# Loading and casting the wide pieces of w_in in parts, with three tiles of the first h side by side

## The chip, the cores and the metric

The kernel runs on one core of one Trainium2 chip. The metric is device microseconds of one execution, as the hardware reports it. The profile of an execution has a "span", from the first to the last instruction, that is about 2.1 us shorter than the reported time.

## The reference

Softmax attention without the score matrix, then a dense layer with exact gelu:

```
q_s = softmax(q, over head_dim);  k_s = softmax(k, over sequence)
kv  = einsum('bhsd,bhse->bhde', k_s, v)          # 8 batches, 8 heads, 64 x 64
x   = einsum('bhsd,bhde->bhse', q_s, kv) -> [4608, 512]
h   = x @ w_in  [512, 2048];  out = gelu(h) @ w_out  [2048, 512]
```

Inputs and output are f32. The kernel computes in bf16 with f32 accumulation.

## The kernel before

The rows of x are worked on in nine chunks of 512. For each chunk there is an h phase (16 tiles of 128 columns of w_in, each the sum of four matmuls, one per "head pair", i.e. per 128 rows of w_in) and a y phase. h tiles live in three PSUM buffers. At the start everything has to be loaded: q, k, v of batch 0, then w_in in five pieces, w_out in four, then batch 1. Each piece is loaded as f32 and cast to bf16.

```python
    psum_h = ctx.enter_context(tc.tile_pool(name="psum_h", bufs=3, space=bass.MemoryType.PSUM))
    ...
    def h_phase(c, ins, group=1, pre={}):
        ...
        for t0 in [0] + list(range(group, NDF)):
            ts = range(t0, t0 + (group if t0 == 0 else 1))
            pss = [psum_h.tile([128, M], FP32, tag="h", name="ps") for t in ts]
            for dm in range(NDM):
                ...
                for ps, t in zip(pss, ts):
                    nc.tensor.matmul(ps, wi_bf[:, dm, t * 128:(t + 1) * 128], xT[:, dm, :],
                                     start=(dm == 0), stop=(dm == NDM - 1))
            for ps, t in zip(pss, ts):
                nc.scalar.activation(out=g[:, t, :], in_=ps, func=AF.Gelu)
                for f in ins.get(t, []):
                    f()
    ...
    wi_cols = [256, 256, 512, 512, 512]      # two narrow pieces, three wide ones
    ...
    warm(30)                                 # matmuls of zeros, to have TensorE's clock up
    ...
    h_phase(0, {0: [lambda: cast_wi(2, wi[2], "v")], 2: [lambda: cast_wi(3, wi[3], "v")],
                4: [lambda: cast_wi(4, wi[4], "v")], ...}, group=2, pre={...})
```

The first wide piece (1 MiB) holds the weights of tiles 4 to 7.

The softmax here doesn't subtract the row's maximum and nothing guards it: scores larger than these inputs give would overflow.

## Time and profile before

| | before |
|---|---|
| three runs, us | 288.55, 288.67, 288.83 |
| span of the profiled one | 286.4 |
| TensorE busy | 277.5 (97%) |
| first wide piece landed / cast whole | 19.64 / 20.89 |
| tile 3 ends / tile 4 starts | 19.72 / 20.95 |
| first y matmul | 31.32 |

TensorE is nearly always busy, so what counts is where it stands still. "Busy" of a matmul goes to its modelled end, which overlaps the next one. I therefore measure a **hold** from start to start: the start of a matmul, less the start of the one before it, less the 0.216 us that follow one another in an undisturbed row. The wait lists of the profile count from the modelled end, so they are about 0.16 us smaller than a hold. A matmul whose record is missing from a trace looks like a hold of 0.216; such places are left out.

### The profile page before, as it was taken

The numbers are of one execution on the slowest core, as the hardware profiler recorded it, in microseconds if no ns is written. First come the engines' busy times: TensorE is split into PE (matmuls) and PEld (weight loads), VectorE is DVE, ScalarE is ACT, GpSimd is POOL, SyncE is SP. The second block draws the span as 40 slices with busy tenths as digits, with TensorE's granted clock in tenths as the row PEclk, the third lists the DMA queues.
The fourth block names the chain that finished last, engine by engine and source line by source line (L and its number), as shares of the span: only waits on it lengthen the run. The fifth ranks groups of instructions, "written<-read, shape, count | busy, mean of one in ns | idle before, by whom it ended". The sixth has DMA issues, their size and how long they took to land.

```text
span 286.4 us, 3707 instructions
## 1 busy us (share of the span) xinstructions
PE 277.5 (97%) x1464; PEld 132.4 (46%) x1491; DVE 116.3 (41%) x211; ACT 153.6 (54%) x211; POOL 38.6 (13%) x34
## 2 busy tenths in 40 slices
PE   8969999999999999999999999999999999999995
PEld 3524455445445445444544454445444444444443
DVE  7654387217694553344324522362225112110012
ACT  5766684779465824584368526761664165016500
POOL 5830033002020050005000500040002200000000
PEclk9999999999999999999999999999999999999999
DMA  7999999998519939922994289616701600120033
GB/s 231 374 382 387 371 389 304 319 292 218 146 45 251 298 105 243 263 82 76 224 282 116 76 187 276 163 73 159 136 2 58 157 7 0 64 83 2 0 72 74
DMA packets 58384, 50.04 MB, mean 175 GB/s; under 512 B 26496, under 2 KB 48256, under 8 KB 58368
## 3 DMA queue, kind: packets, MB, share of 16 engines
q1 hardware_dynamic: 58208, 49.68, 61.3%
q8 instruction: 11, 0.18, 0.3%
q10 hardware_dynamic: 160, 0.13, 0.1%
q14 instruction: 5, 0.04, 0.0%
HBM read 36.70 MB, written 9.44 MB: 161 GB/s over the span
## 4 chain that ended last, share of the span: by engine, by line
PE 89%; DMA 6%; ACT 2%; issue 1%; DVE 1%; SPq 0%; ACTq 0%
PE ps L340 42%; PE ps L350 40%; DMA w<-in_moe_w_in_dram 4%; DMA f<-in_k_dram 2%; PE ps L309 2%; PE ps L237 2%; PE ps L372 1%; ACT ek L152 1%; PE ps L241 0%; ACT L152 0%; DVE wi_bf L416 0%; PE ps L183 0%; ACT e L152 0%; SPq L105 0%; PE ps L314 0%
## 5 line engine op out<-in xcount | busy, mean ns | idle before, releaser
L345 ACT ACTIVATE g<-ps 128x512 bf16<-128x512 f32 x144 | 85.8, 597 | 104.7 <-PE ps L340 104.7
L340 PE MATMUL ps<-xT,wi_bf 128*128 128x512 bf16 x560 | 131.0, 379 | 2.6 <-DVE wi_bf L416 1.2
L350 PE MATMUL ps<-wo_bf,g 128*128 128x512 bf16 x549 | 123.2, 379 | 0.6
L340 PEld LDWEIGHTS <-wi_bf 128*128 128x128 bf16 x576 | 55.5, 98 | 66.8 <-DVE wi_bf L416 1.7
L350 PEld LDWEIGHTS <-g 128*128 128x128 bf16 x560 | 54.6, 98 | 64.9
L357 DVE COPY y_sb<-ps 128x512 f32<-128x512 f32 x35 | 23.9, 688 | 75.6 <-PE ps L350 72.6
L229 POOL TENSOR_TENSOR e<-e,recq 128x1024 bf16<-128x1024 bf16 (+1 forms) x10 | 27.6, 2760 | 179.6 <-DVE recq L228 141.5
L322 DVE CAST xT<-ps 128x512 bf16<-128x512 f32 x33 | 22.8, 691 | 36.2 <-PE ps L309 27.6
L227 DVE TENSOR_REDUCE qsum<-e 128x16 f32<-128x1024 bf16 (+1 forms) x13 | 21.1, 1622 | 9.0 <-ACT e L152 8.9
L152 ACT ACTIVATE e<-f 128x1024 bf16<-128x1024 f32 (+1 forms) x11 | 15.8, 1442 | 4.4 <-DMA f<-in_q_dram 4.3
L210 DVE CAST v_aug<-f 128x512 bf16<-128x512 f32 x24 | 10.3, 429 | 9.9 <-DMA f<-in_v_dram 9.3
L309 PE MATMUL ps<-qT,kvbd 128*128 128x512 bf16 x32 | 12.2, 381 | 0.8 <-ACT kvbd L196 0.6
L94 ACT ACT_TABLE_LOAD x9 | 11.5, 1283 | 0.9 <-PEq L616 0.7
L152 ACT ACTIVATE ek<-f 128x2048 bf16<-128x2048 f32 x6 | 11.4, 1894 | 0.0
L436 PE MATMUL ps<-kvbd 128*128 128x512 bf16 x35 | 10.0, 452 | 1.2 <-DVE scr L82 1.2
L168 ACT ACTIVATE ek<-f 64x1152 bf16<-64x1152 f32 x8 | 9.3, 1162 | 1.7 <-DMA f<-in_k_dram 1.6
L237 PEld LDWEIGHTS <-ek 128*128 128x128 bf16 x96 | 6.8, 97 | 3.1 <-ACT ek L152 0.6
L237 PE MATMUL ps<-v_aug,ek 128*128 128x129 bf16 x96 | 8.1, 220 | 0.1
L152 ACT ACT_TABLE_LOAD x6 | 7.7, 1283 | 0.1
L427 DVE CAST wo_bf<-w 128x2048 bf16<-128x2048 f32 (+1 forms) x5 | 5.1, 1014 | 5.3 <-DMA w<-in_moe_w_out_dram 5.1
L259 DVE TENSOR_TENSOR kvbd<-ps,rec 64x128 bf16<-64x128 f32 x24 | 6.9, 289 | 0.6
L436 PEld LDWEIGHTS <-kvbd 128*128 128x128 bf16 x35 | 3.8, 114 | 6.4 <-issue 2.8
(46 smaller groups left out, 83.7 us busy)
## 6 DMA issues: line engine op xcount, KB each, us to landing
out_dram<-y_sb SPq DMA_DIRECT2D x32, 256.0 KB, 2.4
f<-in_q_dram SPq DMA_DIRECT2D x6, 1024.0 KB, 8.0
f<-in_k_dram SPq DMA_DIRECT2D x6, 1024.0 KB, 10.9
f<-in_v_dram SPq DMA_DIRECT2D x6, 1024.0 KB, 9.9
w<-in_moe_w_in_dram SPq DMA_DIRECT2D x3, 1024.0 KB, 12.5
w<-in_moe_w_out_dram SPq DMA_DIRECT2D x3, 1024.0 KB, 12.2
f<-in_k_dram SPq DMA_DIRECT2D x4, 576.0 KB, 8.3
f<-in_v_dram SPq DMA_DIRECT2D x8, 288.0 KB, 8.5
```

What stands on the lines that cost most here:

```text
L94: nc.scalar.activation(out=scr[:, 1:2], in_=scr[:, 0:1], func=func)
L152: nc.scalar.activation(out=dst[:, i * n:(i + 1) * n], in_=src[:, i * n:(i + 1) * n], func=AF.Exp)
L227: nc.vector.reduce_sum(out=qsum, in_=eq[:, :, hs, :], axis=AX.X)
L229: eng.tensor_tensor(out=eq[:, :, hs, :], in0=eq[:, :, hs, :], in1=recq.unsqueeze(3).to_broadcast([128, J, w, D]), op=ALU.mult,)
L237: nc.tensor.matmul(ps, st[b]["ek"][:, j, hs, :].rearrange("p h d -> p (h d)"), v_aug[b % 2][:, j, hp, 0:PW], start=(j == 0), stop=False,)
L309: nc.tensor.matmul(ps, kvbd[b][:, hp, :], st[b]["qT"][:, :, hp, :], start=True, stop=True)
L322: nc.vector.tensor_copy(out=st[b]["xT"][:, hp, :], in_=ps)
L340: nc.tensor.matmul(ps, wi_bf[:, dm, t * 128:(t + 1) * 128], xT[:, dm, :], start=(dm == 0), stop=(dm == NDM - 1),)
L345: nc.scalar.activation(out=g[:, t, :], in_=ps, func=AF.Gelu)
L350: nc.tensor.matmul(ps, st[c]["g"][:, t, j * 128:(j + 1) * 128], wo_bf[:, t, :], start=(t == 0), stop=(t == NDF - 1),)
L357: nc.vector.tensor_copy(out=y_sb, in_=ps)
L436: nc.tensor.matmul(ps, zeros[:, 0:128], zeros, start=True, stop=True)
```

## The change

Its intent: have the first wide piece usable head pair by head pair as it lands, and have TensorE work on three tiles at once meanwhile, so that the last pair is wanted later.

```diff
-    def h_phase(c, ins, group=1, pre={}):
+    def h_phase(c, ins, groups={}, pre={}):
...
-        for t0 in [0] + list(range(group, NDF)):
-            ts = range(t0, t0 + (group if t0 == 0 else 1))
+        t1 = 0
+        while t1 < NDF:
+            t0, t1 = t1, t1 + groups.get(t1, 1)
+            ts = range(t0, t1)
...
+    wi_parts = [1, 1, 4, 2, 2]
...
-        nc.sync.dma_start(out=w[:, :, 0:n], in_=moe_w_in[...].rearrange("(c p) f -> p c f", p=128))
+        d = NDM // wi_parts[i]
+        for c in range(0, NDM, d):
+            nc.sync.dma_start(out=w[:, c:c + d, 0:n], in_=src[:, c:c + d])
...
-            nc.vector.tensor_copy(out=o, in_=w[:, :, 0:n])
+            for c in range(0, NDM, d):
+                nc.vector.tensor_copy(out=o[:, c:c + d], in_=w[:, c:c + d, 0:n])
...
-        4: [lambda: cast_wi(4, wi[4], "v")],
+        6: [lambda: cast_wi(4, wi[4], "v")],
...
-    }, group=2, pre={
+    }, groups={0: 2, 4: 3}, pre={
```

(The lines with `...` inside brackets are shortened.)

More of the change, by code (lines that the diff above doesn't have):

```diff
@@ L402, in load_wi @@
         n = wi_cols[i]
-        nc.sync.dma_start(
-            out=w[:, :, 0:n],
-            in_=moe_w_in[:, wi_off[i]:wi_off[i] + n].rearrange("(c p) f -> p c f", p=128),
-        )
+        src = moe_w_in[:, wi_off[i]:wi_off[i] + n].rearrange("(c p) f -> p c f", p=128)
+        d = NDM // wi_parts[i]
+        for c in range(0, NDM, d):
+            nc.sync.dma_start(out=w[:, c:c + d, 0:n], in_=src[:, c:c + d])
         return w
@@ L415, in cast_wi @@
         else:
-            nc.vector.tensor_copy(out=o, in_=w[:, :, 0:n])
+            d = NDM // wi_parts[i]
+            for c in range(0, NDM, d):
+                nc.vector.tensor_copy(out=o[:, c:c + d], in_=w[:, c:c + d, 0:n])
     def load_wo(i, parts=1):
@@ L537 @@
         12: [lambda: cast_v_all(2)],
-    }, group=2, pre={
+    }, groups={0: 2}, pre={
         1: [lambda: x_step(1, 3, "s")],
```

## The prediction

> **What bounds the kernel now.** I read the page first, then the waits of TensorE, the chain of waits, and the timeline of the stretch where both agree that TensorE stood still. The page's first part:
>
> ```profile
> PE 277.5 (97%) x1464; PEld 132.4 (46%) x1491; DVE 116.3 (41%) x211; ACT 153.6 (54%) x211; POOL 38.6 (13%) x34
> ```
>
> TensorE is busy for 277.5 of 286.4 us, so a change that adds and removes no matmul can only win the few microseconds in which it stands still. The waits of TensorE over the first 70 us (columns: total us, times, longest) name the ones that the profile sees; from 50 us to the end the same view is empty:
>
> ```profile
> PE ps L340 <- DVE wi_bf L416: 1.2, 1, 1.2
> PE ps L436 <- DVE scr L82: 1.2, 1, 1.2
> ...
> PE ps L340 <- POOL wi_bf L414: 0.4, 1, 0.4
> ```
>
> The largest one inside the work is a matmul of the first h (L340) that waits once for the VectorE cast of a w_in piece (L416). The chain that ended last passes through that same place (start us, us, what):
>
> ```profile
> 8.17 11.47 DMA w<-in_moe_w_in_dram
> ...
> 19.66 1.24 DVE wi_bf L416
> ...
> 20.95 7.30 PE ps L340 x33
> ...
> 31.48 7.55 PE ps L350 x35
> ```
>
> So 1 MiB of w_in, columns 512 to 1023 (tiles 4 to 7), lands at 19.64, is cast whole in 1.24 us, and the first matmul of tile 4 starts at 20.95. From there TensorE runs without a gap, 7.55/35 = 0.2157 us from start to start. The timeline there:
>
> ```profile
> 16.75 2.97 PE L340 MATMUL ps<-xT,wi_bf 128*128 128x512 bf16 x12
> ...
> 17.81 1.68 ACT L345 ACTIVATE g<-ps 128x512 bf16<-128x512 f32 x3 [0.45 <-PE ps L340]
> 19.66 1.23 DVE L416 CAST wi_bf<-w 128x2048 bf16<-128x2048 f32 x1 [2.32 <-DMA w<-in_moe_w_in_dram]
> 19.75 0.60 ACT L345 ACTIVATE g<-ps 128x512 bf16<-128x512 f32 x1 [0.27 <-PE ps L340]
> ...
> 20.95 0.39 PE L340 MATMUL ps<-xT,wi_bf 128*128 128x512 bf16 x1 [1.23 <-DVE wi_bf L416]
> ```
>
> The row of 12 is the end of tiles 0 to 3. It ends at 19.72 and one record is 0.38 long, so its last matmul started at 19.34 and the next could have started at 19.55. It started at 20.95. **1.40 us** is all that this part of the change can win.
>
> **What the Trainium skill says.** "PSUM — Partial Sum Buffer", Specifications: 8 banks per partition, 2 KiB each (512 fp32). A 128x512 f32 tile fills one; the kernel's pools hold 3 (h), 2 (y) and 3 (a), so all 8 are spoken for and h has three banks, no fourth. The trace agrees as far as it goes: no record shows a fourth h tile. "DMA: Bandwidth & Descriptors", Rules for kernel authors, wants at least 1 MiB per DMA for full bandwidth; this trace does not bear that out under a full queue: between 9 and 12.6 us, where v's loads of 288 KB land, the DMA view has 391 GB/s, against a mean of 345 over the first 60 us. So parts of 256 KB should cost no bandwidth. The same page, "Why a DMA increments its semaphore by 16 and not by 1", says that a transfer has landed only when the slowest of its engines has; that a part can be held up by one engine is a risk I keep, although no row shown here measures it.
>
> **The change part by part.**
> Loads: w_in's pieces go from 5 transfers to 10 (1+1+4+2+2), same bytes. The three wide casts start at 19.66, 22.22 and 24.92, so 1 MiB takes about 2.6 us here and a quarter 0.65. The last quarter should land near 19.64 as before, the others, by estimate, near 17.7, 18.35 and 19.0.
> Casts: for the first wide piece one cast of 1.23 becomes four. The cast of w_out takes 0.69 for 1024 columns (two halves) and 1.23 for 2048, so 0.16 plus 0.53 per 1024, and a quarter costs 0.43: 1.7 in all instead of 1.23. VectorE is idle then (2.32 us before the cast), and three of the four lie before 19.55. The last ends near 20.1. The other two pieces cost 2 x 0.69 instead of 1.23 each, beside TensorE; their last halves end 0.5 earlier than the whole did.
> Order on TensorE: tiles 4, 5, 6 alternate over the four head pairs. Pair 3 is wanted only after nine matmuls, 9 x 0.2157 = 1.94 after 19.55, so at 21.5 or later; it is there at 20.1. Hence no wait for weights is left: -1.40.
>
> Side by side, however, needs all three h banks at once. In order of allocation the banks go to: the transposes of q (A), tiles 0 (B), 1 (C), 2 (A), 3 (B), 4 (C), 5 (A), 6 (B), 7 (C). Tile 4 needs tile 1's gelu, tile 5 tile 2's; the row of three gelus ends at 19.49, so both are free. Tile 6 needs tile 3's gelu, which runs from 19.75 to 20.35. A released matmul starts about 0.06 after its releaser (cast end 20.89, matmul 20.95). So:
> - tile 4 pair 0 at 19.55, tile 5 at 19.77, tile 6 not at 19.98 but at 20.41: **+0.43**.
> - The tenth of the twelve, tile 4's last, starts 7 x 0.2157 later, at 21.92, and ends at 22.30; gelu(4) from 22.33 to 22.93. Tile 7 uses its bank: TensorE is free for it at 22.57 and starts at 22.99: **+0.42**.
> - gelu(5) and gelu(6) follow at once and end near 23.5 and 24.1; tiles 8 and 9 want their banks at 23.85 and 24.71: nothing.
> Tile 8 then starts at 22.99 + 4 x 0.2157 = 23.85. Before it was 20.95 + 16 x 0.2157 = 24.40. **The sum is -1.40 + 0.43 + 0.42 = -0.55 us.**
>
> Does it reach the end? Tiles 8 and 12 want weights at 23.85 and 27.3; these end, by the halves, near 22.9 and 25.6. The first y phase comes 0.55 earlier. Its nearest wait is v of batch 1:
>
> ```profile
> 40.44 0.69 DVE L427 CAST wo_bf<-w 128x1024 bf16<-128x1024 f32 x1
> ...
> 42.58 2.95 POOL L174 CAST v_aug<-f 128x576 bf16<-128x576 f32 x4 [3.36 <-DMA f<-in_v_dram]
> ...
> 44.30 0.45 PE L183 MATMUL ps<-v_aug,ek 128*128 128x65 bf16 x9
> ```
>
> The first of four casts ends at 42.58 + 2.95/4 = 43.32 and its matmuls start at 44.30: 0.98 of slack, 0.43 after the shift. w_out's tiles 12 and 13 are cast at 41.13 and used from 42.57: 0.9 left. After that TensorE's wait list is empty, so the gain stays: 288.67 - 0.55 = 288.12.
>
> **The rivals.**
> 1. Nothing of the group costs: -1.40 in h, of which the v cast would take back 1.40 - 0.98 = 0.42, so 287.7. Against it: three banks and a gelu that ends at 20.35. It needs the bank's wait not to be there.
> 2. The wait for the third bank falls on the group's first matmul, not on tile 6's own: tile 4 starts at 20.41 (+0.86), and tile 7's hold of 0.42 remains, 0.12 won, 288.55. For it: nothing in the trace shows a group with a busy bank. Against it: in the timeline each single tile waits for its own bank alone.
> 3. The longer row of DMAs starves the queue. A ninth transfer waits for the first to land:
>
> ```profile
> SPq L403 <- DMA f<-in_k_dram: 1.7, 2, 1.4
> SPq L403 <- DMA f<-in_q_dram: 0.5, 1, 0.5
> ```
>
> With eight in flight, the last w_in half cannot be issued before the second narrow piece lands (15.7 instead of 10.65), and w_out's first not before the first quarter does (17.7 instead of 15.42). At both times, by my count of what was issued and has not landed, 2.5 to 3 MB wait, about 7 us at 390 GB/s, so I expect no hole. If there were one, v of batch 1 would land later by its length, and beyond 0.43 us it would show in full: 288.5 to 289.5.
> 4. A slow engine of the 16 delays one quarter. Pair 3 has 21.5 - 20.1 = 1.4 to spare, the others as much, so this costs nothing unless the delay is well over a microsecond: 288.1 to 288.5.
>
> **Range and chances.** Step 1 (-1.40) I hold firm, since loads and casts have over a microsecond to spare. The two bank holds are arithmetic on durations that repeat within 0.01, but where the wait attaches is assumed; rivals 1 and 2 span 287.7 to 288.55, and the three runs before span 0.28. So 288.1, with 287.4 to 288.7 for 8 in 10. Two per cent is 5.8 us, four times all that is to be won, and a loss of that size would take a starved queue through the whole start: 0.98 within, 0.01 each outside.
>
> **What would show it.** Right: no wait of L340 on a cast of w_in's first wide piece; two waits of L340 on ACT gelu (L345 before) of some 0.2 to 0.4 us each, near 20.0 and 22.6; four casts of about 0.43, the last ending near 20.1; the first y matmul near 30.8 instead of 31.3; the span shorter by 0.55. Wrong: tile 4 starting after 20 (rival 2 or late quarters), a new wait of L183 on POOL's v casts or of L350 on w_out's casts (rivals 1 and 3), or v of batch 1 landing later than 42.5.

## The result, and the profile after

The changed kernel took **288.93 us** (median of four, 288.85 to 289.00), the kernel before 288.75 beside it. The ratio is 1.0005 (95% interval 0.9988 to 1.0023). The prediction of 288.1 with a range up to 288.7 missed.

The first part of the page shows the same 1464 matmuls as before, busy 0.8 us longer (277.5 before):

```profile
PE 278.3 (97%) x1464; PEld 132.8 (46%) x1491; DVE 116.5 (41%) x216; ACT 153.4 (53%) x211; POOL 38.6 (13%) x34
```

The waits of TensorE in the changed kernel no longer list the cast of w_in. In its place stand two on ACT's gelu (total us, times, longest):

```profile
PE ps L342 <- ACT g L347: 0.5, 2, 0.3
...
PE ps L342 <- POOL wi_bf L418: 0.3, 1, 0.3
```

The timeline of the stretch shows where they are:

```profile
17.45 3.40 PE L342 MATMUL ps<-xT,wi_bf 128*128 128x512 bf16 x14
...
17.97 1.42 DVE L422 CAST wi_bf<-w 128x512 bf16<-128x512 f32 x4
...
20.46 0.60 ACT L347 ACTIVATE g<-ps 128x512 bf16<-128x512 f32 x1 [0.27 <-PE ps L342]
...
21.11 2.32 PE L342 MATMUL ps<-xT,wi_bf 128*128 128x512 bf16 x10 [0.26 <-ACT g L347]
...
23.68 7.93 PE L342 MATMUL ps<-xT,wi_bf 128*128 128x512 bf16 x35 [0.25 <-ACT g L347]
...
31.45 10.52 PE L352 MATMUL ps<-wo_bf,g 128*128 128x512 bf16 x47
```

The row of 14 runs through from the second half of tiles 0 and 1 into the first matmuls of tiles 4 and 5, without a gap before tile 4. Tile 6 waits for gelu(3), which ends at 21.06, and tile 7 waits for gelu(4). So the mechanism of the prediction is all there. Yet y starts at 31.45, and before it was 31.32. The chain that ended last now runs through TensorE and gelu(3) where it ran through a DMA and a cast.

The 0.56 us (1.39 less 0.83) that the change should have won here is missing for a reason that lies earlier: all of TensorE's real work up to tile 3 is 0.70 us later. TensorE's own timeline at the start, of the kernel before

```profile
1.19 8.77 PE L436 MATMUL ps<-kvbd 128*128 128x512 bf16 x30 [1.19 <-DVE scr L82]
9.79 0.61 PE L274 MATMUL ps<-identity,e 128*128 128x128 bf16 x8
```

and of the changed kernel:

```profile
1.19 9.47 PE L442 MATMUL ps<-kvbd 128*128 128x512 bf16 x30 [1.19 <-DVE scr L82]
10.49 0.61 PE L274 MATMUL ps<-identity,e 128*128 128x128 bf16 x8
```

The same 30 warm-up matmuls took 8.77 us in one and 9.47 in the other. In the trace's record of the granted clock it went to full at 5.51 us before and at 6.93 after; until then matmuls follow one another every 0.43 us, afterwards every 0.216. The first real work (the transposes, L274) came 0.70 us later. The Trainium skill, "TensorE: Matmul & The Clock Gate", Part 1, says that this release comes at the end of a free-running window of about 3.4 us and varies from run to run. The traces agree that it varies: in the 20 of them it came anywhere from 4.03 to 7.21 us, and late or early in both kernels; the window itself they do not show. So a difference of 0.7 us between two single traces need not be the change's at all. But it had not cost the kernel before anything, if the wait before tile 4 hid it. That became the question.

### The profile page after: what moved, and what is told of

Same layout as the page of the kernel before. It is cut to its first block, busy times and chain, and to the rows that moved or that the text cites. A ratio compares the mean times of both kernels' runs of the same rounds, so it can differ in the third digit from the quotient of the medians.

```text
span 286.8 us, 3717 instructions
## 1 busy us (share of the span) xinstructions
PE 278.3 (97%) x1464; PEld 132.8 (46%) x1491; DVE 116.5 (41%) x216; ACT 153.4 (53%) x211; POOL 38.6 (13%) x34
## 4 chain that ended last, share of the span: by engine, by line
PE 93%; ACT 2%; DVE 2%; issue 1%; ACTq 0%; DVEq 0%
PE ps L342 42%; PE ps L352 40%; PE ps L442 3%; PE ps L309 2%; PE ps L237 2%; PE ps L374 1%; DVE xT L322 1%; ACT ek L152 1%; DVE kvbd L198 1%; PE ps L183 1%; PE ps L241 0%; PE ps L274 0%; ACT L152 0%; ACT g L347 0%; ACT e L152 0%
## 5 line engine op out<-in xcount | busy, mean ns | idle before, releaser
L442 PE MATMUL ps<-kvbd 128*128 128x512 bf16 x35 | 10.7, 476 | 1.2 <-DVE scr L82 1.2
## 6 DMA issues: line engine op xcount, KB each, us to landing
f<-in_v_dram SPq DMA_DIRECT2D x8, 288.0 KB, 8.5
```

The lines of the kernel that those rows point to most:

```text
L442: nc.tensor.matmul(ps, zeros[:, 0:128], zeros, start=True, stop=True)
```

## The experiments

The theories, as the expectations name them. **A**: the group's two waits for a PSUM bank cost 0.84 us; the kernel before hides a late start of TensorE behind the landing of the first wide piece, the changed kernel shows it. **B**: there is no such slack. **C**: the changed program itself delays the clock. **D** (formed after the first four runs): the wait that the change removes is not there in every execution; whether the piece lands at 18.5 or 19.6 us depends on a fetch of instructions that gets in its way, while the group's cost is always there. **E**: what TensorE wins before 74 us is partly taken back by the transpose of batch 2.

Eighteen more runs were made, in five calls, each call on one chip. All gave right results. "Own" are the runs of the kernel before in the same call.

### First call: which part costs, and what does a late start do

**parts_only**

```diff
-    }, groups={0: 2, 4: 3}, pre={
+    }, groups={0: 2}, pre={
```

> Undoes the side-by-side order of tiles 4 to 6, keeps the parts. Theory A (the two waits for an h bank, 0.42 us each, are the cost of the group; and the late start of this execution's TensorE clock is what hid the rest): no wait of the h matmuls on ACT gelu, the 16 h tiles follow at 0.216 us per matmul, and the first y matmul comes 0.84 us earlier than in the changed kernel for the same clock release (about 30.6 if the clock is released near 6.9, about 29.9 if near 5.5). Time about 288.1 (288.0 to 288.3), less what a wait for v of batch 1 takes back (up to 0.4). Rival (the group costs nothing, the parts or their ten transfers do): the time stays at 288.9, y starts at 31.4.

288.43 us (median of six) against 288.36 of its own; ratio 1.0006 (0.9985 to 1.0027); the median lies just above the 288.0 to 288.3 expected. TensorE's timeline:

```profile
17.59 13.33 PE L342 MATMUL ps<-xT,wi_bf 128*128 128x512 bf16 x60
30.76 2.54 PE L352 MATMUL ps<-wo_bf,g 128*128 128x512 bf16 x11
```

One row of 60 matmuls, no hold at tile 4 or after it. The clock came later than ever here (7.21 us), and y still starts 0.69 us earlier than in the changed kernel. The holds belong to the group; the parts and their ten transfers cost TensorE nothing. But only part of that reached the end: y of batch 0 is 0.56 us ahead of the first trace of before, the last y matmul only 0.13 ahead. The difference goes between 74 and 79 us.

**pairs**

```diff
-    }, groups={0: 2, 4: 3}, pre={
+    }, groups={0: 2, 4: 2}, pre={
```

> Tiles 4 and 5 side by side instead of 4 to 6. Theory A: both their banks are free in time (the third bank is not wanted), so no wait on gelu, same as the parts alone within 0.15 us: about 288.1. Rival (any group that ends its tiles together costs a hold at the next tile): some 0.2 to 0.4 us slower than the parts alone.

288.48 us, ratio 1.0008 (0.9982 to 1.0034). Tiles 4 and 5 side by side have no hold, as Theory A had it: two of three banks suffice. The gain of 0.97 us at y again shrinks to 0.63 after 79 us. The timeline there names the reason:

```profile
74.52 0.38 PE L309 MATMUL ps<-qT,kvbd 128*128 128x512 bf16 x1 [0.18 <-DMA qT<-e]
```

The x matmul of batch 2 waits for the transpose by DMA. In the first trace of before that transpose landed at 75.07 and the matmul started at 75.15: a wait of nothing, but a slack of only 0.08 us.

**before_warm34**

```diff
-    warm(30)
+    warm(34)
```

> The kernel before with 34 instead of 30 warm-up matmuls: TensorE's real work starts 4 x 0.216 = 0.86 us later. Theory A (the kernel before hides a late start of TensorE, up to about 1.4 us, behind the landing and cast of w_in's first wide piece): tile 4 still starts at 20.95, y at 31.3 to 31.5, time within 0.2 us of the kernel before. Rival B (there is no such slack, every delay of the start shows): +0.86 us, about 289.6. The clock release of this execution also tells whether the release comes at a fixed 5.5 us for this kernel (rival C: fixed by the program) or varies from execution to execution.

288.18 us, ratio 0.9991 (0.9968 to 1.0014). The timeline of TensorE:

```profile
11.22 0.61 PE L274 MATMUL ps<-identity,e 128*128 128x128 bf16 x8
...
18.17 13.32 PE L340 MATMUL ps<-xT,wi_bf 128*128 128x512 bf16 x60
31.34 1.89 PE L350 MATMUL ps<-wo_bf,g 128*128 128x512 bf16 x8
```

Real work starts 1.43 us later than in the first trace of before (11.22 against 9.79), and y starts 0.02 us later. So the kernel before does absorb a late start: B falls. But it does so without any wait before tile 4. The wide piece landed at 18.57 here, not at 19.64. Nothing in the kernel's loads was changed. This is the observation from which Theory D came.

**after_warm34** (the same edit on the changed kernel)

> The changed kernel with 34 instead of 30 warm-up matmuls. Theory A (with the parts there is no slack left at tile 4, so a late start shows in full): +0.86 us against the changed kernel, about 289.8, y near 32.3 if the clock is released near 6.9 us and near 31.6 if near 5.5. Rival B: the same 0.86, but then the kernel before with 34 has it too. Rival C (the changed program itself delays the clock): release again near 6.9 in this and in the two part kernels.

289.09 us, ratio 1.0027 (1.0007 to 1.0047). Slower, but by less than the 0.86 us expected over the changed kernel of the first comparison. The clock was released at 4.07 us, so C falls: the changed program does not delay it. This execution had its first loads late too (the first narrow piece of w_in at 15.29 instead of 14.24), so its trace cannot size the exposure by itself. Beside before_warm34, with the same edit and on the same chip, the means are 289.11 and 288.14: 0.97 apart. In its trace the kernel before had no wait for the change to remove, so the group's 0.83 us would be most of the difference.

### Second call: repeat both, and move the transpose's competition

**after_again** (no edit)

> The changed kernel once more, unedited, for a second trace and six more times beside runs of the kernel before on the same chip. Theory D (the kernel before seldom has the 1.4 us wait in full: whether w_in's first wide piece lands at 18.5 or 19.6 us depends on whether a 16 KB fetch of instructions, which follows TensorE's progress, falls on one of its DMA engines before or after the piece is through; the group's two bank holds of about 0.3 to 0.4 us are there always): both holds present again (tile 4 to tile 8 takes 0.7 to 0.9 us more than 16 x 0.216 us), the time level with or up to 0.6 us above the kernel before. Rival (the first comparison was unlucky in the clock release and the change is worth its 0.55 us on average): mean 0.4 to 0.7 us below the kernel before.

288.89 us (six runs), ratio 1.0028 (1.0004 to 1.0052). Clock at 4.48 us, so an early TensorE; both holds present, together 0.83. The last part of the wide piece landed at 19.69 and no matmul waited for it. Of the comparisons of the changed kernel as it stands this is the only one whose interval is clear of 1, on the slow side.

**before_again** (no edit)

> The kernel before once more, unedited, for a second trace. Theory D: the clock release differs from 5.5 us; if TensorE comes 0.3 us or more later than in the first trace, the fetch comes later than 17.8 us, the piece lands at 18.4 to 18.7 us and tile 4 follows tile 3 with no wait or at most 0.3 us, at about 20.0 to 20.5. If TensorE comes as early as before or earlier, the fetch falls at 17.5 us or sooner, the piece lands at 19.5 or later, and the wait of 1 us or more is there. Rival: the wait for the cast is there whatever the fetch does, because the piece always lands at 19.6.

288.44 us, ratio 1.0012 (0.9990 to 1.0035) **against itself**. That is the resolution of these comparisons: an unedited copy came out 0.12% apart, inside its interval. In the trace the piece landed at 19.57 and the hold before tile 4 was 1.19 us, as Theory D has it for an early TensorE.

**parts_v3late** (on parts_only)

```diff
-    load(3)
+    load_main(3, "q", q)
+    load_both(3, "k", k)
...
-        (1, 15): [lambda: xbar_step(2)],
+        (1, 15): [lambda: xbar_step(2), lambda: load_both(3, "v", v)],
```

> The parts alone, and v of batch 3 loaded after the transpose of batch 2 instead of before it. Theory E (whatever TensorE wins before 74 us, some 0.4 us of it is taken back there, because the transpose of batch 2 by DMA lands behind the loads of batch 3): the transpose lands 4.2 us or less after its issue and earlier than 74.5, no wait of an x matmul (L309) on it, the gain at y of batch 0 is still there at the end, time 0.4 us below the parts alone, about 287.9 to 288.1. Rival (the transpose takes its 4.4 us by itself): it lands as late as before, and the wait of 0.2 to 0.3 us stays. A later v could also hold up its own casts near 83 us; then a new wait of DVE shows there, but no loss on TensorE unless it exceeds 5 us.

287.97 us, ratio 0.9999 (0.9977 to 1.0020). The transpose took 4.40 us from issue to landing and landed at 74.74, not 4.2 or less and before 74.5 as I expected; in parts_only, pairs, after_again and parts_warm26 it took 4.8 to 4.9. No x matmul waited, and the 0.30 us won by y were still there at the end, where those four lost 0.34 to 0.43. That supports E. It is not the whole story of that wait: before_look below has its v early and its transpose in 4.41 us as well, so the backlog itself varies.

**parts_warm26** (parts_only with `warm(26)`)

> The parts alone with 26 instead of 30 warm-up matmuls: TensorE's real work 0.86 us earlier, down to the limit of the softmax of q (9.2 us). With tile 4 free of its wait nothing holds h before tile 16, so y of batch 0 comes 0.5 to 0.86 us earlier than in the parts alone at the same clock release. Theory E: at most 0.2 us of it reaches the end, since the transpose of batch 2 is already what x waits for (time 288.2 to 288.5). Rival: all of it reaches the end, 287.6 or less.

288.40 us, ratio 1.0013 (0.9993 to 1.0033). y of batch 0 at 30.18, no hold, 1.13 us ahead of the first trace of before; 0.75 of it reached the end, more than the 0.2 of Theory E but not all. The median lies where Theory E put it (288.2 to 288.5), but it is above the 287.78 of its own runs, so the six times do not show the 0.75.

### Third call: move the fetch

**before_warm26** (the kernel before with `warm(26)`)

> The kernel before with 26 instead of 30 warm-up matmuls. Theory D says what makes w_in's first wide piece land at 19.6 instead of 18.5 us is a 16 KB fetch that comes once per about 256 TensorE instructions. Eight instructions fewer (four weight loads, four matmuls) put the fetch at about 19.2 us, as in the parts with 26; then the piece lands at 18.5 to 18.9 us although TensorE is earlier than ever, its cast ends at 19.8 to 20.1 us, tile 4 starts by 20.2 us, and the wait that the change was made for shrinks from 1.2 to below 0.5 us with nothing of the change in it. y of batch 0 at 30.2 to 30.6 us, time 0.3 to 0.6 us below the unedited kernel of this call if the transpose of batch 2 takes the rest. Rival (the fetch has nothing to do with it, the piece is simply that late): lands at 19.5 or later, tile 4 at 20.9, no gain.

288.15 us, ratio 1.0000 (0.9968 to 1.0032). The fetch did move, from 17.45 to 20.00 us, although the transposes started earlier (9.37). The landing did not do what I said: 19.82. In this execution the loads were late from the start (first narrow piece at 15.60, 1.44 later than in the first trace), v's cast held TensorE up for 1.6 us, and the late fetch hit the next wide piece instead, which tile 8 waited for. The traced run was the slowest of its six (289.43). As a test of the landing it failed. What it shows is that the fetch follows the count of TensorE's instructions: with eight fewer in the warm-up it comes later (at 19.2 to 20.0 us in all four traces with 26), and in all 20 traces it comes after 194 to 205 recorded ones.

**parts_v3late_w26** (parts_v3late with `warm(26)`)

> Parts, no group, v of batch 3 after the transpose of batch 2, 26 warm-up matmuls: what the other runs point to. Theories D and E: no bank hold, no wait at tile 4, y of batch 0 near 30.2 to 30.5, none of it lost at 74 us: span 285.4 to 285.7, time 287.4 to 287.7, 0.4 to 1.0 us below the unedited kernel of this call. Rival: another wait (v of batch 1, which lands at 42 to 43 us) takes it back: 288.2 or more.

287.88 us, ratio 0.9984 (0.9953 to 1.0015); y at 30.25, no hold, and of the 1.06 us ahead of the first trace all is still there at 140 us. Inconclusive in the times, taken up again below.

**before_look** (no edit, one run)

> The kernel before, unedited, for a third trace: some of its timed runs were 287.3 to 287.8 us, the two traced ones 288.5. Theory D: if this one is fast, the first wide piece landed near 18.5 us (no fetch on a lagging engine) and tile 4 started by 20.3; if it is near 288.5, the fetch fell before the piece was through and the wait is there.

287.59 us: a fast execution of the unedited kernel. First its VectorE, then its TensorE:

```profile
18.77 1.23 DVE L416 CAST wi_bf<-w 128x2048 bf16<-128x2048 f32 x1 [1.14 <-DMA w<-in_moe_w_in_dram]
```

```profile
17.03 13.56 PE L340 MATMUL ps<-xT,wi_bf 128*128 128x512 bf16 x59
30.43 2.75 PE L350 MATMUL ps<-wo_bf,g 128*128 128x512 bf16 x12
```

The cast starts at 18.77 instead of 19.66, the h tiles run as one row (the hold before tile 4 is 0.22 us, a real one: the first matmul starts 0.05 after the cast's end), and y starts at 30.43, 0.89 us earlier than in the first trace. Of the four traces of the changed kernel only one is earlier there (30.38); the others are at 30.86 and later. All 0.89 us are in the span (285.5 against 286.4). The gain that the change was made for was had here without the change.

### Fourth call: the other half alone, and more executions

**group_only**

```diff
-    wi_parts = [1, 1, 4, 2, 2]
+    wi_parts = [1, 1, 1, 1, 1]
```

> The other half alone: tiles 4 to 6 side by side, loads and casts of w_in whole as in the kernel before. Theory D: the bank holds belong to the group, so tile 4 to tile 8 takes about 0.4 us more than 16 x 0.216 us when tile 4 itself waits for the cast (the bank of tile 6 is free by then, the hold at tile 7 stays) and about 0.8 us more when it does not. Time 0.3 to 0.8 us above the unedited kernel. Rival (the parts cost what the comparison shows and the group is free): level with the kernel before.

288.38 us, ratio 1.0013 (0.9987 to 1.0039). In the trace tile 4 waited 0.17 us for the cast and the group cost another 0.66, together 0.83: a wait in front of the group and the hold inside it overlap, so they do not add. The times cannot tell Theory D from its rival: the interval holds both a level result and 0.39% more.

**before_look2, before_look3, after_look** (no edits, one run each)

> The kernel before, unedited, fourth trace. Theory D: the time goes with the landing of w_in's first wide piece. Landed at 18.8 us or sooner: no wait of tile 4 over 0.2 us, span 285.3 to 285.8. Landed at 19.4 us or later: wait of 0.8 us or more, span 286.3 to 286.6. Rival: the span does not go with that landing.

> The kernel before, unedited, fifth trace; the same two cases as in the fourth: landing by 18.8 us and a span of 285.3 to 285.8, or landing from 19.4 us on and a span of 286.3 to 286.6.

> The changed kernel, unedited, third trace. Theory D: the two holds on the gelu of tiles 3 and 4 are there whatever the landing (tile 4 to tile 8 again 0.8 us over 16 x 0.216), no wait on any cast of the first wide piece even if its last part lands after 19.5 us; span 286.0 to 287.0, going with the start of TensorE's work.

before_look2: 288.54 us, span 286.5, landing at 19.72, but a hold of only 0.38. That is neither of my two cases. Its first loads were late (first narrow piece at 15.52), which delayed TensorE's own early work by as much as the piece. before_look3: 287.33 us, span 285.3, landing at 18.47, hold 0.36. after_look: 288.23 us, span 286.2; last part landed at 19.57, no wait for it, 0.83 in the group.

before_again and after_look are a matched pair: the transposes start at 9.92 and 9.91 us, the piece lands at 19.57 in both. The kernel before:

```profile
20.88 10.53 PE L340 MATMUL ps<-xT,wi_bf 128*128 128x512 bf16 x48 [1.03 <-DVE wi_bf L416]
31.25 2.11 PE L350 MATMUL ps<-wo_bf,g 128*128 128x512 bf16 x9
```

The changed kernel:

```profile
20.52 2.32 PE L342 MATMUL ps<-xT,wi_bf 128*128 128x512 bf16 x10 [0.25 <-ACT g L347]
23.09 7.93 PE L342 MATMUL ps<-xT,wi_bf 128*128 128x512 bf16 x35 [0.25 <-ACT g L347]
30.86 2.32 PE L352 MATMUL ps<-wo_bf,g 128*128 128x512 bf16 x10
```

One wait of 1.03 (a hold of 1.19) is traded for two of 0.25 (holds that sum to 0.83), and y comes 0.39 us earlier; 1.19 - 0.83 = 0.36. In an execution of that kind the prediction's arithmetic holds, with a wait of 1.19 in place of 1.40.

### Fifth call: the means

**before_last, after_last** (no edits) and **best_last** (parts_v3late_w26 again)

> The kernel before, unedited, sixth trace and six times as a control of the comparison itself: against the kernel's own runs of this call a ratio within 0.15% of 1. Theory D: the wait before tile 4 is either 0.2 to 0.4 us (piece landed by 18.8, or TensorE itself late) or 1.2 to 1.4 us (piece landed from 19.5 on with TensorE early), and the span goes with it: 285.3 to 285.8, or 286.3 to 286.6.

> The changed kernel, unedited, fourth trace and six more times. Theory D: no wait before tile 4, 0.83 us more than 16 x 0.216 from tile 4 to tile 8; mean time 0.1 to 0.6 us above the control of this call. Rival (the change is worth its 0.55 us): mean 0.4 us or more below the control.

> Parts without the group, v of batch 3 after the transpose of batch 2, 26 warm-up matmuls, second time: neither wait nor hold, mean time 0.2 to 0.6 us below the control of this call and 0.6 to 1.0 us below the changed kernel.

| | median of six | mean | ratio to own runs |
|---|---|---|---|
| before_last | 288.28 | 288.21 | 0.9995 (0.9974 to 1.0015) |
| after_last | 288.34 | 288.46 | 1.0001 (0.9985 to 1.0017) |
| best_last | 287.43 | 287.62 | 0.9972 (0.9955 to 0.9989) |

The changed kernel is 0.25 us above the control by the means and level with the 11 own runs (288.43): no gain of 0.55. before_last's hold was 0.37, with a landing at 18.89; after_last's group cost 0.83. best_last is the only one of the three whose interval lies clear of 1, and 0.59 below the control as expected; its first run, parts_v3late_w26, was at 0.9984 with an interval that holds 1. It differs from the kernel before in the parts, the later v of batch 3 and the shorter warm-up, and no run shows which of them its gain comes from.

## Why the prediction was wrong

The landing of the first wide piece sorts the executions. "Fetch" is the start of a 16 KB packet of instructions on one of the DMA queues; "narrow" is when w_in's first piece landed; for the changed kernel "wide" is the last of its four parts. Times in us.

| trace | narrow | fetch | wide | hold before tile 4 | in the group |
|---|---|---|---|---|---|
| before | 14.16 | 17.45 | 19.64 | 1.39 | 0 |
| before_again | 14.27 | 17.38 | 19.57 | 1.19 | 0 |
| before_look | 14.56 | 17.60 | 18.74 | 0.22 | 0 |
| before_look2 | 15.52 | 18.71 | 19.72 | 0.38 | 0 |
| before_look3 | 14.29 | 17.53 | 18.47 | 0.36 | 0 |
| before_last | 14.70 | 17.83 | 18.89 | 0.37 | 0 |
| after | 14.24 | 17.92 | 18.40 | 0 | 0.83 |
| after_again | 14.06 | 17.33 | 19.69 | 0 | 0.83 |
| after_look | 14.20 | 17.40 | 19.57 | 0 | 0.83 |
| after_last | 15.32 | 18.49 | 21.03 | 0 | 0.83 |

Where the fetch came by 17.45 the piece landed 5.3 to 5.6 us after the narrow one; where it came at 17.53 or later, 4.2 us after it. The exception, after_last (5.7, with a late fetch), had its loads late by a microsecond, so the piece was still under way when the fetch came; after_warm34, not in the table, is another (5.7, fetch at 18.30). The DMA view shows the fetch as its own queue; in the first trace of before, in the 0.1 us from 17.4 on (packets, MB, share of 16 engines' time):

```profile
q8 instruction: 1, 0.02, 69.5%
```

A share of 69.5% of 16 engines in 0.1 us is 1.11 us of one engine. In that trace 15 of the 16 completions of the piece had come by 18.36 and the last came at 19.64. The Trainium skill, "DMA: Bandwidth & Descriptors", "Why a DMA increments its semaphore by 16 and not by 1", says that only the last completion counts; that trace agrees.

The completions hold a sharper test than the hour of the fetch. In the four late landings other than the exceptions, the fetch started 0.03 to 0.19 us before the first of the 16 completions of the piece (of its last part in the changed kernel); in every other trace it started after it. Where the first wide piece escaped, the delay can turn up in the next one: in before_look3 the sixteenth completion came 0.14 us after the fifteenth in the first wide piece and 0.76 after it in the second. And in after_last one engine was 1.05 us behind the rest at the narrow piece already, before any of this; after the fetch it was 2.55 behind. So an engine can also lag without this fetch. That the fetch is what held the sixteenth engine stays inferred from order and size; no run removed the fetch, and before_warm26, which was meant to move it out of the way, was spoilt by its late loads.

Point by point:

- **"Step 1 (-1.40) I hold firm, since loads and casts have over a microsecond to spare."** This is the step that failed. The 1.40 was right for its trace (1.39) and wrong as a property of the kernel: six traces of before have 1.39, 1.19, 0.22, 0.38, 0.36 and 0.37, mean 0.65. I checked whether the new casts would be in time, and did not ask whether the old wait would be there. "A slow engine of the 16 delays one quarter" was weighed only for the parts; that the same delay had already made the wait in the trace before me was not seen.
- **The two bank holds, +0.43 and +0.42.** Right: 0.83 together in all four traces, and 0 in parts_only and pairs. They were paid in every traced execution. -0.65 + 0.83 is +0.18 us in place of the predicted -0.55. Six waits so far apart give their mean to about 0.2 us (the standard error), so the traces explain why there is no gain, and do not settle whether the sum is a loss. Over all executions of the five calls and the first comparison the means are 288.26 (74 of before) and 288.67 (17 of the changed kernel), a difference of 0.41; in the last call alone it was 0.25 against the control. Chips and calls differ by as much, so what lies beyond the sum stays open.
- **"So the gain stays."** Wrong in part. The wait list of TensorE is empty after 50 us, but an empty list says nothing of slack. The transpose of batch 2 landed 0.08 us before its matmul started, and took back 0.34 to 0.43 us in four traces of edited kernels that came 0.5 us or more earlier. In before_look and before_look3, as early, it took back nothing, and in before_last 0.17, so it depends on the backlog of that execution. With v of batch 3 late, parts_v3late_w26 was 1.06 ahead and lost none of it.
- **The range.** It was built on three runs within 0.28 us of each other. All 74 of the kernel before span 287.26 to 290.23, and 27 of them are below 288.0. In the first comparison the traced execution of the changed kernel started 0.70 us late, which the old wait would have hidden; its three other executions have no trace, so why all four lay within 0.15 us of each other stays open.
- **Loads, casts.** No wait for weights in any changed trace: right. A quarter's cost was mis-sized: 1.42/4 = 0.36 us, not 0.43, and the last cast ended at 19.39, not 20.1. The quarters landed at 16.37, 17.05, 17.73 and 18.40, not at 17.7 to 19.64, since I counted back from a landing that, if the inference above holds, the fetch had delayed.
- **Rival 3 (starved queue)** did not happen: v of batch 1 landed at 42.22, before at 42.52. **Rivals 1 and 2** fall with the holds as measured. **Rival 4** came true as it was told: in after_again, after_look and after_last the last quarter landed 1.8 to 2.2 us after the third, and no matmul waited for it.

## What to carry to other kernels

A wait in one trace is a sample: before spending a fixed cost on it, take several traces and see how often it is there. A group that wanted every buffer of its pool paid twice here, once when its last member waited for the youngest buffer and once when all its members ended together; a group one smaller paid nothing. And an empty wait list is not slack: look how long before its use each late arrival lands.

## What the Trainium skill lacked or had wrong

- "Runtime: NRT & Kernel Launch", "Instruction fetch mechanics", has the size of an instruction fetch (16 KiB), but no page says what a fetch costs the transfers that it meets. Here it is one 16 KB packet; the first one in the span of each trace took 1.09 to 1.13 us, and where it met the first wide piece under a full queue the landing was 1.1 to 1.5 us later.
- "DMA: Bandwidth & Descriptors", Rules for kernel authors, asks for at least 1 MiB per DMA. Under a full queue the 256 KB parts landed 0.67 to 0.68 us apart, some 390 GB/s, no slower than the 1 MiB pieces (2.7 us each).
- "TensorE: Matmul & The Clock Gate", Part 1, says that the ramp costs under 1% and need not be modelled closely. Here its variation (release at 4.03 to 7.21 us) moved the first real matmul by 0.70 us between the first two traces. That is under 1% of the span indeed, and more than the change was worth.
- "PSUM — Partial Sum Buffer" has the eight banks, but not the price of using a pool's last one in a group: 0.83 us for three tiles in three banks, 0 for two.
